# Decode block on one core: the last unit's first value piece ahead of the preceding unit's output mixing

## The chip, the cores and the metric

One core of a Trainium2 chip runs the kernel. The metric is device time in microseconds (us). A run's time is a little longer than the span of its profile, which begins with the first and ends with the last profiled instruction.

## The reference

Two batch rows of width 448 are normalised (`xn`). One branch is attention over the last 4096 positions of a key and value cache, with 16 query heads over 8 key heads of width 256. The other branch is a dense layer with the Mish activation. Both are added to the input:

```python
W = min(4096, max(256, Sk // 4))                 # 4096
q = (xn @ wq) -> (B, 16, 1, 256)
k, v = last W rows of the caches, each head used by 2 query heads
p = softmax(q k^T * 256 ** -0.5)
A = (p v) @ wo
h = xn @ w1 + b1
B = (h * tanh(softplus(h))) @ w2
out = x + A + B
```

Nearly all bytes are keys and values: 2 x 8 x 4096 x 256 bf16 numbers of each, 33.6 MB each. The page counts 77.78 MB moved in all.

## The kernel before, in words

The eight key heads are worked in U = 4 units of two heads, so that a unit holds four pairs of batch row and head. For unit u the keys come in two pieces of 4096 KB (`load_k`, tile `k`, two buffers). The values come in G = 4 pieces of 2048 KB (`load_v`, tile `v`, a ring of three buffers that the query weights and `w1` have used before). All of these large loads are issued by SyncE (SP), in the order of the program, on one queue. A load into a buffer waits on SP until the last reader of that buffer is done, and every load behind it waits too.

The parts of a unit:

- `turns(u, i)` (line 264): VectorE transposes a key piece into `kt`, in the four-byte form.
- `scores(u, i)` (line 329): TensorE (PE) multiplies query and keys, ScalarE (ACT) takes the exponent, and after the second half VectorE lays the weights `p` for the next product.
- `weigh(u)` (line 365): PE sums the weights with a matrix of ones into `dn`, VectorE makes the reciprocal `rec`.
- `values(u, g)` (line 382): 16 matmuls of `p` and value piece g into `pv`, each 32 weight columns by 512. Its last matmul frees the piece's buffer.
- `gather(u)` (line 401): ACT copies `pv` to `vs`, eight matmuls of 8 columns bring it to the transposed output `o`.
- `finish(u)` (line 434): VectorE scales by `rec` into `oT`.
- `relay(u)` (line 446): 16 small matmuls lay `oT` out afresh in `ox_ps`, ACT copies that to `ox`.
- `mix_early(u)` (line 468): eight matmuls of 448 columns with the output weights `wo` add the unit to the row accumulator `early`. Units 0 to 2 are added so.
- `carry()` (line 232): ACT copies `early` to `e_sb`, eight PE instructions put it in the final accumulator `acc`, four groups of 112 columns.

The last unit (u = 3) differs. Its first three value pieces go through `values`, and its fourth piece through `values_fixed` (line 420), which takes the values as the stationary operand and adds straight to `o`; this is 64 matmuls of 8 columns. `mix(3)` and `dense_out` then add to `acc` with 112-column matmuls (line 247). The second dense weight `w2` is loaded in four parts.

The loop body ends, for each unit u of the first three, with `scores(u + 1, 1)`, `weigh(u + 1)`, `relay(u)`, `mix_early(u)`. Below it stand SP's last loads and PE's last work:

```python
u = U - 1
load_v(u, 0)
load_v(u, 1)
load_wo(u)
load_v(u, 2)
load_v(u, 3, 0, 24)
load_v(u, 3, 24, T)
for part in range(len(w2_parts)):
    load_w2(part)
carry()
for g in range(G - 1):
    values(u, g)
```

With three buffers in the ring, value piece 3 of the last unit goes into the buffer that held piece 0 of the same unit. So `load_v(3, 3, 0, 24)` waits on SP for the last matmul of `values(3, 0)`; the second part of that piece and the four parts of `w2` are behind it in SP's program. The engines' programs run in the order written out here; nothing is reordered by a planner.

Of the kernel before, what the change touches and what calls it, by code (L numbers as in the profile page):

```python
# [17 lines left out]
def kernel(  # L18
# [29 lines left out]
    U = Hkv // KU  # L48
# [43 lines left out]
    def load_k(u, r):  # L92
        t = k_pool.tile([P, RK * KE], BF16, tag="k", name="k")
        src = kview[u][:, s0:, :].rearrange("j (c t) d -> c j (t d)", c=C)
        nc.sync.dma_start(out=t[:], in_=src[:, :, r * RK * KE : (r + 1) * RK * KE])  # L95
        k_t[u, r] = t

    def load_v(u, g, lo=0, hi=T):
        if lo == 0:
            v_t[u, g] = ring("v")  # L100
        t = v_t[u, g]
        src = vview[u][:, s0:, :].rearrange("j (g x t) d -> g x j (t d)", g=G, x=C)
        nc.sync.dma_start(  # L103
            out=t[:, lo * Dh : hi * Dh], in_=src[g, :, :, lo * Dh : hi * Dh]
        )

    def load_wo(u):
        w = wo_pool.tile([P, KU, rep, 2 * D], BF16, tag="wo", name="wo")
        if u < U - 1:
            nc.sync.dma_start(  # L110
                out=w[:].rearrange("p k h e -> p (k h e)"),
                in_=A_wo.rearrange("(k u y i) d -> u y k (i d)", k=KU, u=U, i=8)[u],
            )
        for k2 in range(KU if u == U - 1 else 0):
            r0 = (u + U * k2) * rep * Dh
            nc.sync.dma_start(
                out=w[:, k2, :, :],
                in_=A_wo[r0 : r0 + rep * Dh, :].rearrange("(h p c) d -> p h (c d)", h=rep, p=P),
            )
        wo_t[u] = w  # L120
# [111 lines left out]
    def carry():  # L232
        e_sb = small.tile([P, 2 * Dh], FP32, tag="vs", name="e_sb", bufs=1)[0:Bsz, 0:D]
        nc.scalar.copy(out=e_sb, in_=early[:])
        for g in range(G):
            nc.tensor.matmul(
                acc[32 * g : 32 * g + Bsz, :],
                lhsT=id2[:],
                rhs=e_sb[:, g * DG : (g + 1) * DG],
                start=True,  # L240
                stop=False,
                skip_group_check=True,
            )
# [20 lines left out]
    def turns(u, i):  # L264
        t = k_t.pop((u, i))
        for r in range(RK):
            nc.vector.transpose(  # L267
                out=kt[i][:, :, :, r, :],
                in_=t[:, r * KE : (r + 1) * KE].bitcast(FP32).rearrange(
                    "p (a c j) -> p a c j", c=P // (R * J), j=J  # L270
                ),
            )
# [56 lines left out]
    def scores(u, i):  # L329
        if i == 0:  # L330
            state["ex"] = small.tile([P, T, 2, NH, RK * J], BF16, tag="ex", name="ex", bufs=1)
        ex = state["ex"]
        sc = ps_sc.tile([P, T, 2, RK * J], FP32, tag="sc", name="sc")
        nc.tensor.matmul(  # L334
            sc[:].rearrange("p t c m -> p (t c m)"),
            lhsT=ident[:],
            rhs=mneg[:].rearrange("p a j -> p (a j)"),
            start=True,
            stop=False,
            skip_group_check=True,  # L340
        )
        for n in range(NB):
            for e in range(2):
                for w in range(4):
                    nc.tensor.matmul(  # L345
                        sc[32 * w : 32 * (w + 1)].rearrange("p t c m -> p t (c m)"),
                        lhsT=qd[:, u, 2 * n + e, :, :].rearrange("p g q -> p (g q)"),
                        rhs=ktm[i][:, n, e, :, 16 * w : 16 * (w + 1)],
                        start=False,
                        stop=(n == NB - 1 and e == 1),  # L350
                        skip_group_check=True,
                    )
        nc.scalar.activation(out=ex[:, :, :, i, :], in_=sc[:], func=ACT.Exp, scale=scale)  # L353
        if i == NH - 1:
            for h in range(NH):
                nc.vector.transpose(  # L356
                    out=p_t[h][:].rearrange("p g t q -> p t g q"),
                    in_=ex[:, h * TH : (h + 1) * TH].rearrange(
                        "p t c i m -> p t (c i m)"
                    ).rearrange("p t (g q) -> p t g q", g=G),  # L360
                )
# [20 lines left out]
    def values(u, g):  # L382
        if g == 0:
            state["v", u] = ps_v.tile([P, 2, Dh], FP32, tag="v", name="pv")
        pv = state["v", u]
        v = v_t.pop((u, g))
        for k in range(T // 2):
            a, b = k // 2, k % 2
            w = 2 * (a % 2) + b
            nc.tensor.matmul(  # L390
                pv[32 * w : 32 * (w + 1), :, :].rearrange("p x d -> p (x d)"),
                lhsT=p_t[a // 4][:, g, 4 * (a % 4) : 4 * (a % 4) + 4, :].rearrange(
                    "p t q -> p (t q)"
                ),
                rhs=v[:, 2 * k * Dh : (2 * k + 2) * Dh],
                start=(g == 0 and a < 2),
                stop=(g == G - 1 and a >= 6),
                skip_group_check=True,
            )

    def gather(u, last=True):
        pv = state.pop(("v", u))
        sb = small.tile([P, 2, Dh], FP32, tag="vs", name="vs", bufs=1)
        nc.scalar.copy(  # L404
            out=sb[:].rearrange("p x d -> p (x d)"), in_=pv[:].rearrange("p x d -> p (x d)")
        )
        po = ps_o.tile([P, 2, NQ], FP32, tag="o", name="o")
        for x in range(2):
            for c in range(2):
                nc.tensor.matmul(  # L410
                    po[:, c, :],
                    lhsT=sb[:, x, c::2],
                    rhs=sel[:, x, :],
                    start=(x == 0 and c == 0),
                    stop=(last and x == 1),
                    skip_group_check=True,
                )
        state["o", u] = po
# [27 lines left out]
    def relay(u):  # L446
        oT = state.pop(("oT", u))
        ox_ps = ps_m.tile([P, 4, 2, Bsz], FP32, tag="m", name="ox_ps")
        for h in range(rep):
            rows = slice(h * 64, (h + 1) * 64)  # L450
            for y in range(4):
                for k in range(KU):
                    nc.tensor.matmul(
                        ox_ps[rows, y, :, :],
                        lhsT=hot[:, k, y, :, :].rearrange("p q k -> p (q k)"),
                        rhs=oT[:, :, k * rep + h, :],
                        start=(y == 0 and k == 0),
                        stop=(y == 3 and k == KU - 1),
                        skip_group_check=True,
                    )  # L460
        ox = small.tile([P, 8, Bsz], BF16, tag="ox", name="ox")
        nc.scalar.copy(  # L462
            out=ox[:].rearrange("p i b -> p (i b)"),
            in_=ox_ps[:].rearrange("p y c b -> p (y c b)"),
        )
        state["ox", u] = ox

    def mix_early(u):
        ox = state.pop(("ox", u))
        w = wo_t.pop(u)[:].rearrange("p k h (c d) -> p (k h c) d", c=2)  # L470
        for i in range(8):
            nc.tensor.matmul(  # L472
                early[:],
                lhsT=ox[:, i, :],
                rhs=w[:, i, :],
                start=False,
                stop=(u == U - 2 and i == 7),
            )
# [87 lines left out]
    for u in range(U - 1):  # L566
        load_k(u + 1, 0)
        load_v(u, 0)
        load_v(u, 1)
        load_k(u + 1, 1)  # L570
        load_v(u, 2)
        load_v(u, 3)
        load_wo(u)
        turns(u + 1, 0)
        values(u, 0)
        values(u, 1)
        scores(u + 1, 0)
        turns(u + 1, 1)
        values(u, 2)
        values(u, 3)  # L580
        gather(u)
        finish(u)
        scores(u + 1, 1)
        weigh(u + 1)
        relay(u)
        mix_early(u)
    u = U - 1
    load_v(u, 0)
    load_v(u, 1)
# [3 lines left out]
    load_v(u, 3, 24, T)  # L593
    for part in range(len(w2_parts)):
        load_w2(part)
    carry()
    for g in range(G - 1):
        values(u, g)
    u = U - 1
    gather(u, last=False)  # L600
    values_fixed(u, G - 1, 0, 24)
# [45 lines left out]
```

The softmax here doesn't subtract the row's maximum and nothing guards it: scores larger than these inputs give would overflow.

## Time and profile before

| what | value |
|---|---|
| time, median of 3 runs | 194.07 us (193.81 to 194.4) |
| time of the profiled execution | 194.2 us |
| its span | 192.0 us |
| PE busy | 88.5 us (46%) |
| VectorE busy | 89.3 us (47%) |
| ACT busy | 12.3 us (6%) |
| HBM read | 77.67 MB, 405 GB/s over the span |
| SP's value loads, waiting for a DMA to land | 82.9 us in 12 waits |
| SP's value loads, waiting for PE | 33.2 us in 13 waits |
| last matmul of `values(3, 0)` ends | 175.86 us |
| `load_v(3, 3, 0, 24)` issued | 175.88 us |

How to read it: no compute engine is busy for half of the span, and the DMA engines are busy in nearly all of it. Busy time is a mean over the span; what a change is worth is read from the stretch in which it stands, here the last 25 us. In the view of stretches of time, each row gives a stretch, its length, each engine's busy time with the number of instructions, then the granted clock of PE, the busy share of the 16 DMA engines and what they moved. A DMA packet is counted there where it starts, so that a share can pass 1.

### The profile page before, as it was taken

The numbers are of one execution on the slowest core, as the hardware profiler recorded it, in microseconds if no ns is written. First come the engines' busy times: TensorE is split into PE (matmuls) and PEld (weight loads), VectorE is DVE, ScalarE is ACT, GpSimd is POOL, SyncE is SP. The second block draws the span as 40 slices with busy tenths as digits, with TensorE's granted clock in tenths as the row PEclk, the third lists the DMA queues.
The fourth block names the chain that finished last, engine by engine and source line by source line (L and its number), as shares of the span: only waits on it lengthen the run. The fifth ranks groups of instructions, "written<-read, shape, count | busy, mean of one in ns | idle before, by whom it ended". The sixth has DMA issues, their size and how long they took to land.

```text
span 192.0 us, 1986 instructions
## 1 busy us (share of the span) xinstructions
PE 88.5 (46%) x870; PEld 37.1 (19%) x873; DVE 89.3 (47%) x81; ACT 12.3 (6%) x23; POOL 4.0 (2%) x16
## 2 busy tenths in 40 slices
PE   0301554553238023866354034964380038788472
PEld 0100121520112001412111011511130014222261
DVE  5629544965960295029910691059700970130001
ACT  3000121001001000110001001010001001101101
POOL 8000000000000000000000000000000000000000
PEclk9999999558556755567558555585567555675855
DMA  6999998999999999999999999999999999997990
GB/s 219 437 386 434 492 437 360 452 420 420 423 440 437 427 425 417 443 434 423 447 440 396 413 424 480 423 393 430 478 430 393 416 432 435 401 415 294 311 412 15
DMA packets 5871, 77.78 MB, mean 405 GB/s; under 512 B 868, under 2 KB 1640, under 8 KB 2408
## 3 DMA queue, kind: packets, MB, share of 16 engines
q1 hardware_dynamic: 5588, 77.66, 96.0%
q8 instruction: 6, 0.10, 0.2%
q10 hardware_dynamic: 276, 0.01, 0.1%
q14 instruction: 1, 0.01, 0.0%
HBM read 77.67 MB, written 0.00 MB: 405 GB/s over the span
## 4 chain that ended last, share of the span: by engine, by line
DMA 79%; PE 11%; DVE 3%; issue 3%; SPq 2%; ACT 1%; DVEq 0%; ACTq 0%
DMA v<-in_A_v_cache_dram 58%; DMA k<-in_A_k_cache_dram 15%; DMA w<-in_B_w_dram 5%; PE pv L390 5%; DVE kt L267 2%; PE sc L345 2%; PE early L472 1%; PE o L410 1%; DVE p L356 1%; SPq L103 1%; SPq L544 1%; SPq L132 1%; SPq L95 1%; ACT ex L353 0%; ACT vs L404 0%
## 5 line engine op out<-in xcount | busy, mean ns | idle before, releaser
L267 DVE STREAM_TRANSPOSE kt<-k 128x4096 f32<-128x4096 f32 x16 | 70.1, 4420 | 40.7 <-DMA k<-in_A_k_cache_dram 40.6
L390 PE MATMUL pv<-v,p 128*32 128x512 bf16 x240 | 27.3, 608 | 56.7 <-DMA v<-in_A_v_cache_dram 56.7
L345 PE MATMUL sc<-kt,qd 128*32 128x512 bf16 x256 | 26.4, 582 | 4.6 <-DVE kt L267 2.3
L390 PEld LDWEIGHTS <-p 128*32 128x32 bf16 x240 | 8.7, 128 | 73.7 <-issue 66.0
L437 DVE TENSOR_TENSOR oT<-o,rec 128x16 bf16<-128x16 f32 x4 | 0.7, 176 | 31.4 <-PE o L410 16.6
L356 DVE STREAM_TRANSPOSE p<-ex 128x512 bf16<-128x512 bf16 x8 | 5.2, 690 | 15.9 <-ACT ex L353 15.9
L345 PEld LDWEIGHTS <-qd 128*32 128x32 bf16 x256 | 8.4, 131 | 19.2 <-issue 16.9
L353 ACT ACTIVATE ex<-sc 128x512 bf16<-128x512 f32 x8 | 4.8, 597 | 74.6 <-PE sc L345 74.6
L289 PE MATMUL q_ps<-wq,xs 128*32 128x512 bf16 x28 | 3.4, 624 | 11.9 <-DMA wq<-in_A_wq_dram 11.9
L472 PE MATMUL early<-wo,ox 128*2 128x448 bf16 x24 | 7.8, 491 | 0.8 <-ACT ox L462 0.8
L410 PE MATMUL o<-sel,vs 128*128 128x8 f32 x32 | 6.7, 339 | 2.8 <-ACT vs L404 2.8
L410 PEld LDWEIGHTS o<-sel,vs 128*128 128x128 f32 x32 | 6.4, 293 | 6.0 <-ACT vs L404 6.0
L368 PE MATMUL dn<-p,ones 128*128 128x512 bf16 x8 | 3.1, 381 | 6.6 <-DVE p L356 6.6
L404 ACT COPY vs<-pv 128x512 f32<-128x512 f32 x4 | 2.3, 586 | 51.8 <-PE pv L390 51.8
L502 PE MATMUL h_ps<-xs,w 128*128 128x4 bf16 x49 | 2.8, 193 | 4.6 <-DMA w<-in_B_w_dram 4.6
L210 PE MATMUL xr_ps<-ident,xrows 2*128 2x2 bf16 x7 | 1.0, 182 | 6.7 <-DVE xrows L209 6.7
L502 PEld LDWEIGHTS <-w 128*128 128x128 bf16 x49 | 2.7, 152 | 5.2 <-DMA w<-in_B_w_dram 5.2
L289 PEld LDWEIGHTS <-xs 128*32 128x32 bf16 x28 | 1.0, 125 | 13.9 <-issue 13.9
L376 DVE TENSOR_REDUCE rec<-dn 128x8 f32<-128x512 f32 x4 | 2.8, 692 | 1.9 <-PE dn L368 1.9
L425 PE MATMUL o<-p,v 128*128 128x8 bf16 x64 | 1.9, 168 | 2.5 <-DMA v<-in_A_v_cache_dram 2.5
L472 PEld LDWEIGHTS <-ox 128*2 128x2 bf16 x24 | 2.2, 102 | 4.1 <-issue 2.1
L334 PE MATMUL sc<-mneg,ident 128*128 128x512 bf16 x5 | 3.0, 591 | 0.0
(62 smaller groups left out, 36.3 us busy)
## 6 DMA issues: line engine op xcount, KB each, us to landing
k<-in_A_k_cache_dram SPq DMA_DIRECT2D x8, 4096.0 KB, 30.4
v<-in_A_v_cache_dram SPq DMA_DIRECT2D x15, 2048.0 KB, 27.3
wo<-in_A_wo_dram SPq DMA_DIRECT2D x3, 896.0 KB, 24.0
wq<-in_A_wq_dram SPq DMA_DIRECT2D x1, 2048.0 KB, 16.8
w<-in_B_w_dram SPq DMA_DIRECT2D x1, 1568.0 KB, 32.2
wq<-in_A_wq_dram SPq DMA_DIRECT2D x1, 1536.0 KB, 19.9
v<-in_A_v_cache_dram SPq DMA_DIRECT2D x1, 1536.0 KB, 7.1
wo<-in_A_wo_dram SPq DMA_DIRECT2D x2, 448.0 KB, 15.6
```

Of the source, the lines that this page charges most:

```text
L267: nc.vector.transpose(out=kt[i][:, :, :, r, :], in_=t[:, r * KE : (r + 1) * KE].bitcast(FP32).rearrange("p (a c j) -> p a c j", c=P // (R ...
L289: nc.tensor.matmul(q_ps[32 * u : 32 * (u + 1), :], lhsT=xs[:, s, :], rhs=wq_t[s][:, u * 512 : (u + 1) * 512], start=(s == 0), stop=(s == N ...
L334: nc.tensor.matmul(sc[:].rearrange("p t c m -> p (t c m)"), lhsT=ident[:], rhs=mneg[:].rearrange("p a j -> p (a j)"), start=True, stop=Fal ...
L345: nc.tensor.matmul(sc[32 * w : 32 * (w + 1)].rearrange("p t c m -> p t (c m)"), lhsT=qd[:, u, 2 * n + e, :, :].rearrange("p g q -> p (g q) ...
L353: nc.scalar.activation(out=ex[:, :, :, i, :], in_=sc[:], func=ACT.Exp, scale=scale)
L356: nc.vector.transpose(out=p_t[h][:].rearrange("p g t q -> p t g q"), in_=ex[:, h * TH : (h + 1) * TH].rearrange("p t c i m -> p t (c i m)" ...
L368: nc.tensor.matmul(dn[:].rearrange("p a q -> p (a q)"), lhsT=ones[:], rhs=p_t[i][:].rearrange("p g t q -> p (g t q)"), start=(i == 0), sto ...
L376: nc.vector.tensor_reduce(out=rec[:], in_=dn[:].rearrange("p a q -> p q a"), axis=AXIS.X, op=ALU.add)
L390: nc.tensor.matmul(pv[32 * w : 32 * (w + 1), :, :].rearrange("p x d -> p (x d)"), lhsT=p_t[a // 4][:, g, 4 * (a % 4) : 4 * (a % 4) + 4, :] ...
L410: nc.tensor.matmul(po[:, c, :], lhsT=sb[:, x, c::2], rhs=sel[:, x, :], start=(x == 0 and c == 0), stop=(last and x == 1), skip_group_check ...
L472: nc.tensor.matmul(early[:], lhsT=ox[:, i, :], rhs=w[:, i, :], start=False, stop=(u == U - 2 and i == 7),)
L502: nc.tensor.matmul(h_ps[:, i, :, :].rearrange("p k b -> p (k b)"), lhsT=w1_v[:, s, i, :], rhs=xs[:, s, 0 : 2 * Bsz], start=(s == 0), stop= ...
```

## The change

The last trip of the loop no longer issues `relay(2)` and `mix_early(2)`. Both are issued after `values(3, 0)`, and `carry()` with them, ahead of `values(3, 1)`:

```diff
@@ -582,8 +582,9 @@
         finish(u)
         scores(u + 1, 1)
         weigh(u + 1)
-        relay(u)
-        mix_early(u)
+        if u < U - 2:
+            relay(u)
+            mix_early(u)
     u = U - 1
     load_v(u, 0)
     load_v(u, 1)
@@ -593,9 +594,12 @@
     load_v(u, 3, 24, T)
     for part in range(len(w2_parts)):
         load_w2(part)
-    carry()
     for g in range(G - 1):
         values(u, g)
+        if g == 0:
+            relay(u - 1)
+            mix_early(u - 1)
+            carry()
     u = U - 1
     gather(u, last=False)
     values_fixed(u, G - 1, 0, 24)
```

On PE, 16 matmuls of `values(3, 0)` pass 16 of `relay(2)`, 8 of `mix_early(2)` and 8 of `carry`. The number of instructions on every engine stays the same. The orders of VectorE, ACT, GpSimd and SP stay as they were: the ACT copies `ox` and `e_sb` follow one another as before, and SP's loads have the same order and wait for the same things.

## The prediction

> **What bounds the kernel now.** I read three views: the chain that ended last, the waits of SP's queue, and half-microsecond stretches of the last 20 us. The chain, in order of time (start, length, what), from the place of the change on:
>
> ```profile
> 168.81 0.38 PE dn L368
> 169.19 0.51 PE ox_ps L453 x16
> 169.69 0.02 issue
> 169.72 0.18 ACT ox L462
> ...
> 169.94 2.86 PE early L472 x8
> ...
> 172.88 0.53 ACT e_sb L234
> ...
> 173.45 0.55 PE acc L236 x8
> 174.00 1.86 PE pv L390 x9
> 175.86 0.02 issue
> 175.88 0.54 SPq L103
> ...
> 178.26 10.52 DMA w<-in_B_w_dram
> ```
>
> The end hangs on the transfers of `w2`. They were issued behind a load (line 103) that SP could issue only when `values(3, 0)` had read its buffer. Those 16 matmuls stood behind 4.81 us (169.19 to 174.00) of relay, mix and carry. That SP waits for PE here, and PE for values, the waits say (total us, times, longest):
>
> ```profile
> SPq L103 <- PE pv L390: 33.2, 13, 10.4
> ```
>
> What the late issue costs the DMA engines (the last three columns: granted clock, DMA share, GB/s):
>
> ```profile
> 174.50:175.00 0.50, 0.50 (x12) 0.16 (x4) 0.00 (x0) 0.00 (x0) 0.00 (x0) 0.50 1.23 524
> 175.00:175.50 0.50, 0.50 (x8) 0.16 (x4) 0.00 (x0) 0.00 (x0) 0.00 (x0) 0.50 0.47 197
> 175.50:176.00 0.50, 0.50 (x8) 0.16 (x4) 0.00 (x0) 0.00 (x0) 0.00 (x0) 0.50 0.46 197
> 176.00:176.50 0.50, 0.50 (x12) 0.19 (x8) 0.00 (x0) 0.00 (x0) 0.00 (x0) 0.50 0.31 131
> 176.50:177.00 0.50, 0.50 (x12) 0.23 (x5) 0.00 (x0) 0.00 (x0) 0.00 (x0) 0.50 0.08 33
> 177.00:177.50 0.50, 0.39 (x8) 0.04 (x1) 0.00 (x0) 0.00 (x0) 0.00 (x0) 0.88 1.25 295
> ...
> 187.00:187.50 0.50, 0.24 (x16) 0.24 (x16) 0.00 (x0) 0.00 (x0) 0.00 (x0) 0.50 0.64 215
> 187.50:188.00 0.50, 0.30 (x16) 0.12 (x5) 0.00 (x0) 0.00 (x0) 0.00 (x0) 0.50 0.11 22
> 188.00:188.50 0.50, 0.00 (x0) 0.00 (x0) 0.00 (x0) 0.00 (x0) 0.00 (x0) 0.50 0.06 20
> ```
>
> The hole is not a clean one. More than half of the 16 engines stop near 175.4, the rest run out one after another until about 177.1: the transfer ahead, `v(3, 2)`, ends late on some engines. PE sees it only then:
>
> ```profile
> 177.60 1.05 PE L390 MATMUL pv<-v,p 128*32 128x512 bf16 x16 [0.21 <-DMA v<-in_A_v_cache_dram]
> ...
> 188.83 0.55 PE L247 MATMUL acc<-w,act_bf 128*2 128x112 bf16 x12 [1.03 <-DMA w<-in_B_w_dram]
> ```
>
> At the very end a share of 0.06 is one engine of 16: a single engine holds the last two parts of `w2`, and PE waits 1.03 us for it.
>
> **What the Trainium skill says.** "DMA: Bandwidth & Descriptors", section on queues, rings and completion order: one queue is a ring on each engine, consumed in ring order; so work queued early follows on each engine at once. The section on why a DMA increments its semaphore by 16 says that the engines finish independently and only the full count means landed. The trace agrees: `v(3, 2)` counts as landed at 177.6, though most engines stopped some 2 us before. "Runtime: NRT & Kernel Launch", section on instruction fetch mechanics: an engine's program is refilled in blocks of 16 KiB by a DMA queue of its own. The page lists 6 instruction packets on q8 with 0.10 MB, which is 16 KB each. I read the late engines, and the single one at the end, as those that had to fetch such a block; that is an inference, as the views name no engine.
>
> **The change part by part.** No instruction is added or removed.
>
> *The values piece.* `dn` ends at 169.19. `v(3, 0)` was issued at 140.77 and took 24.6 us to land, so it is there at 165.4. `pv` is free since ACT's copy at 160.87, and `p` since 168.77. So `values(3, 0)` runs from 169.19 for 1.86 us (its time here at half clock; 1.05 us at full clock, as at 177.60). It ends at 171.05 at the latest, 4.81 us earlier.
>
> *SP.* `load_v(3, 3, 0, 24)` goes out at 171.1 instead of 175.88. The second part and the four parts of `w2` follow, 3.3 us of issue in all (175.88 to 179.22 in before), so that all six are queued by 174.4. They also need semaphores that `v(3, 1)` and the first half of `wo(3)` last used. The latter is the later one: issued 155.97, 15.6 us to land, 171.6. It bars the last part alone, which comes up at 174. All bytes are then queued before the first engine runs dry near 175.4. The cover is some 4 us wide: the first load could go out as late as 174 or so.
>
> *Relay, mix and carry* move 1.86 us later and take the same 4.81 us: 171.05 to 175.86. `values(3, 1)` begins at 175.9 as before, and PE is ready for `values(3, 2)` at 177.4 as before, where it waits for `v(3, 2)` until 177.6. ACT's two copies have nothing behind them until `vs` at 178.75. The buffers of `wo(2)`, `ox` and `e_sb` come free later, but nobody waits for them. Cost: nothing, with 0.2 us of cover; beyond that, each us is lost to `gather`, which is not the bound.
>
> *What is late next.* `v(3, 2)` is not moved, so the engine that finishes it at 177.1 goes on there. Behind it are 2048 KB of `v(3, 3)` and 1568 KB of `w2`, in all 3.70 MB, or 231 KB for each engine. In before these took three steps:
> - first part of `v(3, 3)`, 1.57 MB: 177.0 to 182.0 at a mean of 315 GB/s (ten stretches, 98 to 393), 5.0 us;
> - the other 2.13 MB at 404 GB/s (182.0 to 187.0): 5.3 us;
> - 0.4 us to land, and the single late engine, to 178.7 + 10.3 = 189.0 for the last part (the longest time to landing against its issue), some 1.25 us behind the others' 177.1 + 5.0 + 5.3 + 0.4 = 187.8.
>
> In after, the single late engine need not count. If its fetch falls on an engine that is not late with `v(3, 2)`, that engine has up to 1.7 us in hand (175.4 against 177.1), and the 1.25 us vanish.
>
> The slow first part is the unknown. If the stop and common restart make it slow, it takes 1.57 MB / 420 GB/s = 3.75 us, the rate of the stretches before the hole. If its 12-KB rows do, it stays at 5.0 us. I take 4.4: with engines out of step, the late ones have part of it to themselves. Then the last `w2` lands at 177.1 + 4.4 + 5.3 + 0.4 = 187.2, against 189.0: 1.8 us gained. The bounds are 186.55 (2.5 gained) and 187.8 (1.2 gained).
>
> *PE as the bound.* With `v(3, 3)` landing near 181.9, PE does 1.87 (line 425), 0.26 (VectorE and hand-over), 0.92 (`mix`), then 0.82, 0.54 and 0.55 for `dense_out`: 4.96 us, to 186.9, even with no pause. That is before 187.2 + 0.35, so DMA stays the bound, narrowly. `gather` at half clock would end by 182.1 (1.9, 0.6 and 1.9 from 177.6) and set 187.05.
>
> **Sum.** 1.8 us of the profiled execution's own 194.2 us: 192.4. Its span goes from 192.0 to 190.2. The profiled execution lies 0.13 us above the median of 194.07, within its runs' spread, so I leave the number as it is, rounded down to 192.3.
>
> **Rivals.**
> - *A, the forecast:* late engines carry on at once, fetch hidden; 191.7 to 193.0. Chance 0.64.
> - *B, the fetch hits a late engine:* then the 1.25 us stay. With the first part at 4.4 us the gain is 0.55; over its bounds, 0 to 1.25. Time 192.9 to 194.2, mean 193.6. For it: several engines are late, and one more fetch will come. Against: `v(3, 2)` ends on the late engines step by step, as if each had lost one fetch and none two. Chance 0.18, about half of it over 0.3% faster.
> - *C, the late engines don't matter:* if all ran level, 175.4 + 3.75 + 5.3 + 0.4 = 184.85, and PE's 186.5 to 187.0 would be the end; 191.5. Against: `v(3, 2)` itself is not issued earlier. Chance 0.06.
> - *D, slower:* the low rate of 177 to 182 is that of engines out of step, and as nothing brings them into step any more, it holds to the end. Place: DMA from 177.1. It decides below 3.70 MB / (189.0 - 0.4 - 177.1 us) = 322 GB/s; at 300 GB/s the last part lands at 189.8, 0.8 later: 195.0. For it: 315 GB/s was measured in this very stretch. Against: before the hole, with engines out of step too, it was over 400. Chance 0.07.
> - *E, it does not do what it says:* SP is held by something else, for example the landing of `v(3, 0)`, and issues as late as before: 194.2. Chance 0.05.
>
> **How the numbers follow.** 0.3% of 194 us, 0.58 us, is about what can be told from no change here. Faster: 0.64 + 0.06 + 0.12 of B (its larger part, as a fetch that is partly hidden falls there too) = 0.82. Within: the rest of B and E, 0.11. Slower: D, 0.07. The range reaches from C's 191.5 to B's upper part, 193.9; outside lie D, E and the last of B, some 0.16.
>
> **What would show it.** In the profile of the changed kernel: line 390 right after `dn` near 169.2; SP's load at 170.4 to 171.1, all six issues done by 174.5; no stretch between 175 and 177.5 with a DMA share under 0.8; `v(3, 2)` landing at 177.6 still; the 64 matmuls of line 425 starting near 181.3 to 182.2 in place of 183.02; no wait of a full microsecond for `w` ahead of the last matmuls. I'd be wrong if `v(3, 2)` landed later than 178 because the earlier engines' new traffic slows the late ones; if the stretch from 177 to 182 still moved some 315 GB/s and the last `w2` still landed on one engine alone; or if PE, and not `w2`, were what ends last.

## The result and the profile after

| | before | changed |
|---|---|---|
| median, us | 194.24 (4 runs) | 191.85 (4 runs, 191.77 to 191.99) |
| ratio to before | 1 | 0.987 (95% interval 0.9829 to 0.9911) |
| profiled execution, us | 194.2 | 191.77 |
| its span, us | 192.0 | 189.5 |
| load of the fourth value piece issued at | 175.88 | 171.21 |
| last part of `w2` landed at (its issue and its time to landing) | 189.0 | 186.3 |

The changed kernel is faster by 1.3%. A second set of six runs, shown with the experiments, gave 191.86 us and a ratio of 0.9879 (0.985 to 0.9908). The kernel before has two groups of runs, 53 of its 84 in all sets between 192.59 and 194.66 us and 31 between 194.82 and 195.8, so its median moves with their mix, while the ten runs of the changed kernel lie within 191.72 to 191.99.

The chain that ended last, of the changed kernel (start, length, what), beginning where `dn` ends:

```profile
168.16 1.17 PE dn L368 x2
169.34 1.86 PE pv L390 x16
171.20 0.02 issue
171.21 0.54 SPq L103
...
172.49 0.54 SPq L544
173.04 0.05 issue
173.09 12.37 DMA w<-in_B_w_dram
185.45 0.04 issue
185.49 0.54 PE acc L247 x11
```

Relay, mix and carry have left the chain: `pv` follows `dn` at once, and SP issues 4.67 us earlier. A part of `w2` now stands in the chain for 12.37 us (the second part), where one stood for 10.52 in before (the third). That is no loss: it is queued earlier and waits behind other bytes.

What PE waited for on the way, in the changed kernel:

```profile
177.55 1.05 PE L390 MATMUL pv<-v,p 128*32 128x512 bf16 x16 [0.21 <-DMA v<-in_A_v_cache_dram]
181.26 1.86 PE L425 MATMUL o<-p,v 128*128 128x8 bf16 x64 [0.81 <-DMA v<-in_A_v_cache_dram]
```

Half-microsecond stretches of the changed kernel (the last three columns: granted clock, DMA share, GB/s), at the place of the hole and at the end:

```profile
175.00:175.50 0.50, 0.33 (x1) 0.00 (x0) 0.00 (x0) 0.08 (x1) 0.00 (x0) 0.80 0.99 418
175.50:176.00 0.50, 0.01 (x1) 0.01 (x2) 0.00 (x0) 0.44 (x1) 0.00 (x0) 1.00 1.04 442
176.00:176.50 0.50, 0.50 (x12) 0.21 (x16) 0.00 (x0) 0.00 (x0) 0.00 (x0) 1.00 1.14 483
176.50:177.00 0.50, 0.50 (x16) 0.26 (x9) 0.00 (x0) 0.00 (x0) 0.00 (x0) 1.00 0.70 295
177.00:177.50 0.50, 0.34 (x8) 0.05 (x1) 0.00 (x0) 0.00 (x0) 0.00 (x0) 1.00 1.11 467
...
184.00:184.50 0.50, 0.39 (x24) 0.21 (x16) 0.00 (x0) 0.00 (x0) 0.00 (x0) 0.50 0.73 264
184.50:185.00 0.50, 0.50 (x28) 0.50 (x26) 0.00 (x0) 0.00 (x0) 0.00 (x0) 0.50 0.36 143
185.00:185.50 0.50, 0.25 (x15) 0.06 (x3) 0.00 (x0) 0.00 (x0) 0.00 (x0) 0.50 0.35 131
185.50:186.00 0.50, 0.50 (x16) 0.35 (x16) 0.00 (x0) 0.00 (x0) 0.00 (x0) 0.50 0.22 74
```

The hole is gone: the five stretches from 175 have a mean share of 1.0 (a packet counts where it starts, so 0.70 and 1.11 belong together). The end has a new look. From 184.5 on, about six of the 16 engines (0.36 of them) still work, for some 1.5 us, while the others have finished. Just as many worked on alone in the hole of before (a share of 0.46 and then 0.31, up to 176.5), so I take them for the engines that were late with `v(3, 2)`; the views name no engine. In before, the stop let the others wait for them.

The rate behind `v(3, 2)`, as one stretch of 5 us of each kernel, before first, then changed:

```profile
177.00:182.00 5.00, 2.55 (x32) 1.42 (x24) 0.00 (x0) 0.59 (x1) 0.00 (x0) 0.84 0.97 315
```

```profile
176.00:181.00 5.00, 3.50 (x48) 1.90 (x48) 0.00 (x0) 0.59 (x1) 0.00 (x0) 1.00 0.98 408
```

In both the engines were busy (0.97 and 0.98), but they moved 315 GB/s in one and 408 in the other. The packets of the trace say it row by row: the 128 rows of 12 KB took 0.61 us each in before, on the mean, and 0.465 in the changed kernel; for an engine's eight rows that is some 1.1 us. So a slow period followed the hole.

### The profile page after: what moved, and what is told of

Same layout as the page of the kernel before. It is cut to its first block, busy times and chain, and to the rows that moved or that the text cites. A ratio compares the mean times of both kernels' runs of the same rounds, so it can differ in the third digit from the quotient of the medians.

```text
span 189.5 us, 1989 instructions
## 1 busy us (share of the span) xinstructions
PE 93.9 (50%) x873; PEld 38.0 (20%) x873; DVE 89.2 (47%) x81; ACT 12.3 (7%) x23; POOL 4.0 (2%) x16
## 4 chain that ended last, share of the span: by engine, by line
DMA 81%; PE 9%; DVE 3%; issue 3%; SPq 2%; ACT 1%; DVEq 0%
DMA v<-in_A_v_cache_dram 59%; DMA k<-in_A_k_cache_dram 15%; DMA w<-in_B_w_dram 7%; PE pv L390 5%; DVE kt L267 2%; PE sc L345 2%; PE o L410 1%; PE acc L247 1%; PE dn L368 1%; SPq L103 1%; SPq L132 1%; SPq L95 1%; DVE p L356 0%; ACT ex L353 0%; ACT vs L404 0%
## 5 line engine op out<-in xcount | busy, mean ns | idle before, releaser
L390 PE MATMUL pv<-v,p 128*32 128x512 bf16 x240 | 26.2, 583 | 53.7 <-DMA v<-in_A_v_cache_dram 53.7
L345 PE MATMUL sc<-kt,qd 128*32 128x512 bf16 x256 | 28.2, 614 | 3.2 <-DVE kt L267 1.8
L472 PE MATMUL early<-wo,ox 128*2 128x448 bf16 x24 | 9.4, 570 | 0.8 <-ACT ox L462 0.8
L368 PE MATMUL dn<-p,ones 128*128 128x512 bf16 x8 | 4.3, 540 | 6.0 <-DVE p L356 6.0
L334 PE MATMUL sc<-mneg,ident 128*128 128x512 bf16 x8 | 4.8, 595 | 0.0
L453 PEld LDWEIGHTS <-hot 128*64 128x64 bf16 x48 | 2.0, 142 | 2.6 <-issue 2.6
```

The lines of the kernel that those rows point to most:

```text
L334: nc.tensor.matmul(sc[:].rearrange("p t c m -> p (t c m)"), lhsT=ident[:], rhs=mneg[:].rearrange("p a j -> p (a j)"), start=True, stop=Fal ...
L345: nc.tensor.matmul(sc[32 * w : 32 * (w + 1)].rearrange("p t c m -> p t (c m)"), lhsT=qd[:, u, 2 * n + e, :, :].rearrange("p g q -> p (g q) ...
L368: nc.tensor.matmul(dn[:].rearrange("p a q -> p (a q)"), lhsT=ones[:], rhs=p_t[i][:].rearrange("p g t q -> p (g t q)"), start=(i == 0), sto ...
L390: nc.tensor.matmul(pv[32 * w : 32 * (w + 1), :, :].rearrange("p x d -> p (x d)"), lhsT=p_t[a // 4][:, g, 4 * (a % 4) : 4 * (a % 4) + 4, :] ...
L472: nc.tensor.matmul(early[:], lhsT=ox[:, i, :], rhs=w[:, i, :], start=False, stop=(u == U - 2 and i == 7),)
```

## Experiments

The theory under test, "stop and restart": the time hangs on whether the last loads are queued before the DMA engines run dry, and on nothing else that the change does. Rivals: the order or the clock of PE; the amount of the delay, microsecond for microsecond; the shape of the transfer that follows.

### The wait taken away in the old order, and in the new

```diff
-            v_t[u, g] = ring("v")
+            if (u, g) == (U - 1, G - 1):
+                v_t[u, g] = k_pool.tile([P, RK * KE], BF16, tag="k", name="v")
+            else:
+                v_t[u, g] = ring("v")
```

The fourth piece lies in a key buffer; `values_fixed` reads the first KE columns of it. On the kernel before:

> The kernel before in its own order of work, but the fourth value piece of the last unit lies in a key buffer that is free by 158 us, so that SP's load waits for no value piece and goes out near 161. Theory 'stop and restart': the hole at 175 to 177 is gone and the time is that of the changed kernel, 191.5 to 192.1. Rival 'PE' (the order on PE or its clock brings the gain): 194.2, or the hole is gone and the end is not earlier by over 0.5 us.

On the changed kernel:

> The changed kernel with that same key buffer for the fourth value piece. If freeing the buffer earlier is all that the change does, it has nothing left to bring: the time is that of the kernel with the own buffer in the old order, 191.5 to 192.1, within 0.3 us. If the order on PE is worth something by itself, this one is faster than the other by over 0.5 us.

Measured: 191.71 us, ratio 0.9899 (0.986 to 0.9937), and 191.84 us, ratio 0.9904 (0.9871 to 0.9937). SP's issues in the first of them (start, length):

```profile
160.94 1.25 SPq L106 DMA_DIRECT2D v<-in_A_v_cache_dram  x2
162.29 9.69 SPq L547 DMA_DIRECT2D w<-in_B_w_dram  x4
```

Issued 15 us earlier, in the old order of PE, the kernel takes what the changed one takes, and the new order adds nothing to it. The order on PE is worth something only through the buffer that it frees. The rival "PE" falls.

### How early is early enough

Three kernels put the load at other times. The changed kernel with relay alone back ahead of `values(3, 0)`:

```diff
+        relay(u)
         if u < U - 2:
-            relay(u)
             mix_early(u)
...
         if g == 0:
-            relay(u - 1)
             mix_early(u - 1)
             carry()
```

> The changed kernel, but relay(2) goes back ahead of values(3, 0), with its copy on ScalarE; mix and carry stay behind. SP's load goes out some 0.6 us later than in the changed kernel, near 171.8. Theory 'stop and restart': still 3 us before the engines run dry, so the time is that of the changed kernel, 191.8 within 0.3. Rival 'amount of delay' with no free cover: 0.5 us slower, 192.4.

The kernel before with relay and five matmuls of mix ahead, and three of mix and carry behind (`mix_early` takes bounds for this):

```diff
         relay(u)
-        mix_early(u)
+        mix_early(u, 0, 8 if u < U - 2 else 5)
...
-    carry()
     for g in range(G - 1):
         values(u, g)
+        if g == 0:
+            mix_early(u - 1, 5, 8)
+            carry()
```

> The changed kernel, but relay(2) and five of the eight matmuls of mix_early(2) stay ahead of values(3, 0); three of mix_early and carry stay behind. SP's load goes out near 173.9, 2.7 us later than in the changed kernel and about 1.1 earlier than with carry alone moved, which cost 1.7 us. Theory 'stop and restart': it is still in time, or just so, for first bytes at 175.2, and costs nothing or little: 191.7 to 192.3. Rival 'amount of delay': 1 us or more is lost, 192.8 to 193.2.

The kernel before with only carry behind:

```diff
-    carry()
     for g in range(G - 1):
         values(u, g)
+        if g == 0:
+            carry()
```

> The kernel before, with only carry moved behind values(3, 0); relay and mix stay ahead of it. SP's load should go out near 174.7 us, 1.2 earlier than in before and 3.5 later than in the changed kernel. Theory 'stop and restart' (the gain is that bytes are queued before the DMA engines run dry, and that no common restart follows): the first engines run dry near 175.4 and the new bytes start near 176.0, so about ten engines pause for 0.6 us and the late ones not at all; the stretch from 176 to 181 should move 380 GB/s or more, and the time be 191.9 to 192.8. Rival 'amount of delay' (each us of earlier issue is a us of time, until 2.4 are gained): 1.2 us gained, 193.0. Rival 'PE' (the gain is PE's order or clock at the end): as before, 194.2.

| load issued at (profiled execution) | kernel | median, us | ratio to before (95%) |
|---|---|---|---|
| 160.94 | old order, own buffer | 191.71 | 0.9899 (0.986 to 0.9937) |
| 171.21 | changed | 191.85 | 0.987 (0.9829 to 0.9911) |
| 172.06 | mix and carry behind | 191.82 | 0.9881 (0.9833 to 0.9928) |
| 173.09 | three of mix and carry behind | 192.28 | 0.9898 (0.9855 to 0.994) |
| 175.04 | carry behind | 193.54 | 0.9955 (0.9919 to 0.999) |
| 175.88 | before | 194.24 | 1 |

It is a step with a slope, not a line: 11 us of further delay from the first row to the third cost nothing, the next 1 us costs 0.3 to 0.5, and between 173.09 and 175.88 the rest of the gain is lost. The rival "amount of delay" falls for early issues and is not far off for late ones, with 2 us lost over the last 2.8 us of delay. How the loss divides over the last rows is not settled, since the issue time in the row of carry belongs to an execution of 194.57 us, 1 us above the median, and its twelve runs reach down to 191.59, where the changed kernel is. My own expectation for carry alone was 191.9 to 192.8, as the late engines have no pause in it; that was too good by 0.4 us (by its ratio, 193.2) to 0.7 us (by its median). The missing part is in the rate, and the kernel with five matmuls ahead shows it (columns as above):

```profile
175.00:176.00 1.00, 0.61 (x12) 0.20 (x5) 0.00 (x0) 0.00 (x0) 0.00 (x0) 1.00 1.04 401
176.00:177.00 1.00, 0.00 (x0) 0.00 (x0) 0.00 (x0) 0.00 (x0) 0.00 (x0) 1.00 0.93 389
177.00:178.00 1.00, 0.42 (x8) 0.23 (x11) 0.00 (x0) 0.00 (x0) 0.00 (x0) 1.00 1.05 406
178.00:179.00 1.00, 0.63 (x12) 0.12 (x4) 0.00 (x0) 0.27 (x1) 0.00 (x0) 1.00 1.00 332
179.00:180.00 1.00, 0.63 (x4) 0.64 (x4) 0.00 (x0) 0.31 (x1) 0.00 (x0) 0.75 0.84 279
```

There is no hole here: the share stays near 1 from 175 to 179. Yet from 178 on the rate falls to 332 and then 279 GB/s. A load that comes just in time still costs something, so a full stop of all engines is not what makes the slow period.

### Is it the shape of what follows?

The old order with the fourth piece in one DMA, so in 16-KB rows:

```diff
-    load_v(u, 3, 0, 24)
-    load_v(u, 3, 24, T)
+    load_v(u, 3)
```

> The kernel before, but the fourth value piece of the last unit is loaded by one DMA (16-KB rows) in place of two (12-KB and 4-KB rows); the stop at 175 to 177 stays. It asks why the first 1.57 MB after the stop moved at 315 GB/s. Theory 'common restart' (whatever follows a stop is slow for some 5 us): the stretch from 177 to 182 moves 300 to 340 GB/s again, and the time is 194 to 195. Rival '12-KB rows in step' (only this shape is slow, when all engines begin it together): the stretch moves 400 or more, w2 lands 1.3 us earlier, and the time is 192.7 to 193.3, though values_fixed begins later, as it waits for the whole piece.

Measured: 193.1 us, ratio 0.9927 (0.9892 to 0.9963); from 177 to 182 the engines moved 390 GB/s. That is the rival's time, and nearly its rate. But in this run `values(3, 0)` was at full clock, and the load went out at 174.56, 1.3 us earlier than in before, so the earlier issue could have done it. The two kernels without `mix(3)`, shown below, settle that: they load the piece in 12-KB and 4-KB rows, their loads went out at 174.94 and 174.74, and they are as slow as before. The same stretch with 16-KB rows, then in those two:

```profile
177.00:182.00 5.00, 2.92 (x24) 2.14 (x23) 0.00 (x0) 0.59 (x1) 0.00 (x0) 0.71 0.97 390
177.00:182.00 5.00, 2.71 (x24) 1.92 (x23) 0.00 (x0) 0.58 (x1) 0.00 (x0) 0.78 0.98 327
177.00:182.00 5.00, 2.90 (x24) 2.11 (x23) 0.00 (x0) 0.58 (x1) 0.00 (x0) 0.74 0.95 310
```

So 16-KB rows suffer less than 12-KB rows do.

The old order with `w2` first, in the buffer that `values(3, 0)` frees, and the fourth piece behind it in the key buffer:

```diff
-            state["w2"] = k_pool.tile([P, RK * KE], BF16, tag="k", name="w2")
+            state["w2"] = ring("w2")
...
+    for part in range(len(w2_parts)):
+        load_w2(part)
     load_v(u, 3, 0, 24)
     load_v(u, 3, 24, T)
-    for part in range(len(w2_parts)):
-        load_w2(part)
```

> The kernel before, in its order of work, with two buffers exchanged and SP's last loads turned round: the four parts of w2 go into the ring buffer that values(3, 0) frees, and follow it, and the fourth value piece goes into the free key buffer behind them. The stop near 175 to 177 stays, but what follows it is w2, rows that lie end to end in memory. It asks whether the slow stretch belongs to the stop or to the value piece. Theory 'common restart': w2 is slow too, the 3 us after the restart move 300 to 340 GB/s. Rival 'the value piece's rows': w2 moves at 390 or more, and the value piece, if anything, is slow behind it. The time says little, as the 64 matmuls of values_fixed and mix now come after the last byte: 194.5 to 196.5 is expected either way.

Measured: 196.64 us, ratio 1.0118 (1.0079 to 1.0156), just above what was expected; the load of `w2` went out at 174.92. The rate after the restart, with `w2` first:

```profile
176.00:177.00 1.00, 0.00 (x0) 0.00 (x0) 0.00 (x0) 0.00 (x0) 0.00 (x0) 1.00 0.59 182
177.00:178.00 1.00, 0.40 (x8) 0.23 (x11) 0.00 (x0) 0.00 (x0) 0.00 (x0) 1.00 0.88 351
178.00:179.00 1.00, 0.64 (x12) 0.12 (x4) 0.00 (x0) 0.25 (x1) 0.00 (x0) 1.00 1.04 368
179.00:180.00 1.00, 0.61 (x5) 0.62 (x5) 0.00 (x0) 0.33 (x1) 0.00 (x0) 0.92 0.88 331
```

The mean from 177 to 180 is 350 GB/s, between what the two theories gave, and in each full stretch under the 390 of the rival. Put together: every transfer that followed a late issue was slower than the 408 GB/s of the changed kernel, by some 4% (16-KB rows), 14% (`w2`, where a share of 0.93 is a part of it) and 20 to 24% (12-KB rows). The same 12-KB rows ran at 408 when they had been queued in time. So the shape sets how much. What sets whether is less sharp than the name "late issue" says: in the kernel with `w2` first, the fourth piece went out at 177.26 and its first rows began 3 us later, at 180.3, and still the engines, at a share of 0.98, moved only 370 GB/s from 181 to 185. These are single traces. What inside the DMA system makes the rows slow was not found, and stays open.

### The single late engine at the end

In before, one engine landed the last two parts of `w2` a good microsecond behind the others, and I took it for the one that fetched PE's last program block. The kernel before without `mix(3)`, which leaves out the last unit's product with `wo`:

```diff
     finish(u)
-    mix(u)
```

> The kernel before without mix(3): the last unit's product with the output weights is left out, 32 matmuls on PE (with their weight loads 64 instructions) that lie beside DMA in before. Theory 'instruction fetch' (the single engine that lands the last two parts of w2 some 1.25 us late is the one that fetched PE's last program block): with 64 instructions fewer behind it the fetch starts later, when w2 has landed or nearly, so the last part lands at 187.8 and the time is near 193.0; the instruction packet then lies after 187.5. If the fetch still starts before 187, no change is expected from either side. Rival 'slow engine or small last parts': the last part lands at 189.0 as before and the time is 194.0.

And with idle matmuls ahead of the first `weigh`, which restore the length of the program:

```diff
+        for i in range(32 if u == 0 else 0):
+            nc.tensor.matmul(
+                dn[:, 0, :], lhsT=ones[:], rhs=p_t[0][:, 0, 0, :], start=True, stop=True
+            )
```

> The same without mix(3), and with 32 short matmuls of no use (64 instructions) ahead of the first weigh, where PE has time, so that the program is as long again as that of before and its last block begins at the old distance from the end. Theory 'instruction fetch': the packet is back at 184 to 187 and one engine lands late, 1.2 us behind the others; the time is near 194.2, slower by about 1 us than without the padding. Rival: the two differ by less than 0.3 us.

Measured: 194.12 us, ratio 0.9992 (0.9968 to 1.0017) without the padding, and 193.58 us, ratio 0.9952 (0.993 to 0.9974) with it. The direction was the opposite of what I expected, as the instruction packet didn't go where I had put it. Without `mix(3)` it lies between 185 and 187, as in before, so that this kernel could not decide. With the padding there are two, one between 174 and 176, inside the hole, and one after 188, when all has landed. PE's last lines, without padding and with it:

```profile
186.79 0.54 PE L247 MATMUL acc<-w,act_bf 128*2 128x112 bf16 x16 [0.25 <-DMA w<-in_B_w_dram]
188.09 0.51 PE L247 MATMUL acc<-w,act_bf 128*2 128x112 bf16 x12 [0.77 <-DMA w<-in_B_w_dram]
```

```profile
187.49 1.09 PE L247 MATMUL acc<-w,act_bf 128*2 128x112 bf16 x28 [0.27 <-DMA w<-in_B_w_dram]
```

With the padding PE no longer waits ahead of the last parts. But that is no proof that they came earlier: PE was 0.7 us later here (187.49 against 186.79), and it began the last 12 matmuls at 188.03, against 188.09 without the padding. Nor does the time decide. The difference of 0.5 us between the medians comes mostly from 8 of the 20 unpadded runs, at 194.99 us and more, while no padded run is above 194.25; the other twelve have a median of 193.69 us, and the two profiled executions, 193.43 and 193.36 us, are alike. What speaks for the fetch is in the packets. In before the instruction packet runs from 186.44 to 187.33, and from 187.3 to 188.1 four rows of 1792 bytes, each begun where the last ended and so on one engine, take 0.19 to 0.20 us each, where such rows take 0.074 elsewhere; that engine then works on alone to the end. Without `mix(3)` it is the same (packet from 186.04 to 187.0, and two such rows of 0.20 from 187.0 on), and with the padding, where no packet falls on the tail, no row is slow. So the fetch as the cause of the lone engine is supported by the packets, while its worth in time is not shown.

### The same padding on the changed kernel

> The changed kernel with the 32 short matmuls of no use (64 instructions) ahead of the first weigh, as in the padded one before, so that PE's program blocks are fetched at other times. Theory 'stop and restart': a fetch that delays one engine by about 1.2 us is hidden, since late engines 1.5 us behind decide the end: 191.8 within 0.3. Rival 'every fetch near the end counts': the time moves by 0.5 us or more, either way.

Measured: 191.37 us, ratio 0.9843 (0.9802 to 0.9885). That is outside what my theory gave (191.5 to 192.1), by little. As the changed kernel had been measured in another set, both were run again side by side:

> The changed kernel itself, as the neighbour of the padded one on the same chip: 191.6 to 192.1.

> The changed kernel with the 32 short matmuls of no use, a second time, beside the changed kernel itself. In the trace of the changed kernel PE does one matmul of the last two parts of w2 at 186.07 and the next at 186.48, with no wait that the profile shows; in the padded one they run on. Theory 'program block' (the edge of a program block falls there, and the padding moves it): 0.3 to 0.5 us faster than its neighbour, 191.3 to 191.5. Rival 'chip or day': no difference over 0.2 us.

Measured: 191.86 us, ratio 0.9879 (0.985 to 0.9908), and padded 191.41 us, ratio 0.9855 (0.9823 to 0.9888); the runs are 191.72 to 191.92 and 191.16 to 191.59, with no overlap. PE's last two groups in the timeline, without padding and with it:

```profile
185.59 0.83 PE L247 MATMUL acc<-w,act_bf 128*2 128x112 bf16 x17 [0.24 <-DMA w<-in_B_w_dram]
186.60 0.45 PE L247 MATMUL acc<-w,act_bf 128*2 128x112 bf16 x11 [0.18 <-issue]
```

```profile
185.51 1.11 PE L247 MATMUL acc<-w,act_bf 128*2 128x112 bf16 x28 [0.25 <-DMA w<-in_B_w_dram]
```

Without the padding PE pauses before 186.60 with no wait that the profile shows; with it the 28 matmuls run through and end near 186.62, against 187.05. This 0.4 us is the difference, 0.08 of it an earlier start. It is a pause in PE's own program, not in a transfer; that it is the edge of a program block is inferred from what moves it. It lies behind the same matmul in six other traces of unpadded kernels, those of the two with an own buffer and of all with the load at other times among them. It is missing in the padded ones, but also in before and in the kernel with one DMA for the piece, so the place in the program alone does not make it. The padded version is the fastest of the study, though by an accident of length that any later edit can undo.

## Why the prediction was right

The forecast was 192.3 us, and 191.85 was measured. By its steps:

- *The values piece and SP's issue.* `values(3, 0)` ran from 169.27 and ended at 171.20; the load went out at 171.21 and all six were issued by 174.45. Forecast: 171.05 at the latest, 171.1 and 174.4. Right but for 0.15 us, as `dn` ran at half clock here and ended at 169.34.
- *Relay, mix and carry at no cost.* PE waited for `v(3, 2)` until 177.55 as before, and relay, mix and carry lay ahead of it. Right. The cover was given as some 4 us and as reaching to an issue at 174, which do not agree, for 174 is only 2.9 us behind 171.1. It is 1 to 2 us: 172.06 is free, 173.09 costs 0.3 to 0.5.
- *No stretch under a share of 0.8.* By the letter this sign failed, with 0.70 at 176.5; together with the 1.11 behind it there is no hole.
- *The late engines decide.* `v(3, 2)` was seen by PE at 177.55 against 177.60, so it didn't move, and about six engines worked on alone at the end. Right; rival C, that they don't matter, needed the last landing at 184.85, and it was at 186.3. That late engines are those that had to fetch a block stayed an inference, but it fits in number: in before, six instruction packets (five of q8, one of q14) lie between the start of the span and the hole.
- *The first part's rate.* I took 4.4 us, between 3.75 and 5.0. This is the term that was mis-sized: at 408 GB/s its 1.57 MB take 3.85 us. The 64 matmuls of line 425 began at 181.26, at the early edge of the stretch named. The reason for 4.4, that engines out of step keep part of the slowness, was wrong; transfers queued in time had none of it.
- *The fetch.* One instruction packet falls between 184 and 185 in the changed kernel, too. The last `w2` landed at 186.3 on several engines together, with no lone one behind; the 1.25 us vanished, as said, and rival B did not come. The landing was forecast for 187.2, with 186.55 as the fast bound; it was earlier than that bound by 0.25 us.
- *PE close behind.* 186.9 was worked out for an uninterrupted PE with the fourth piece landing near 181.9. The piece came 0.7 us earlier, and PE's last matmul still ended at 186.93, by a pause of 0.4 us that I hadn't seen coming. So the sign "if PE, and not `w2`, were what ends last" came true for that last bit; without the pause the gain would have been 2.8 us.
- *Rival D*, that engines out of step stay slow, is refuted: they moved 408 GB/s out of step. *E* is refuted by the issue at 171.21.

The sum then reads: 1.25 us from the lone engine, 1.15 us from the rate of the first part (5.0 to 3.85), and some 0.3 us that no term accounts for, which makes 2.7 us at the last landing (189.0 to 186.3); PE's pause took some of it back, and 2.5 us of span are left. The mechanism was right. That the total fell on the fast bound of 2.5 us is in part luck, since the early landing and the pause, neither of them forecast, nearly cancel.

## What to carry to other kernels

Where the DMA queue is the bound, look for stretches in which the engines run out, and follow SP back to the instruction that frees the buffer; moving that one reader ahead of work that nobody waits for gained some 2 us here. By the sum above the idle time itself was not the gain, since ten engines now only finish earlier and the six late ones set the end; the gain was what followed the hole, the slow rows and the lone engine. Queue the next loads a few microseconds before the last ones end, as a load that is just in time already costs: here an issue at 172.06, 3.3 us before the first engines ran dry in before (175.4), was free, and one at 173.09, 2.3 us before, was not. And read the last microseconds by number of engines: a share of 0.06 is one late engine, and 0.36 is six.

## What the runs showed that I had not expected

- After a late issue the DMA engines are busy but slow: 315 GB/s at a share of 0.97 for 5 us, against 408 at 0.98. It happens with the share never under 0.8 too (332 and 279 GB/s in the kernel with five matmuls ahead). Only the transfer that comes first was slow in before: of the rows behind its 12-KB ones, those of 4 KB took 0.159 us in before and 0.161 in the changed kernel.
- 32 matmuls of no use, at 8 columns each, make the changed kernel 0.45 us faster, with a pause in PE's program gone from the path.
- The time at which the buffer comes free depends on PE's clock. In before the load went out at 175.88, with `values(3, 0)` at half clock (1.86 us). In the kernel without `mix(3)`, the same up to there, it was 174.94, with the clock at 1.0 from 173. Once the load is early, this no longer reaches the end: four runs of the changed kernel lie within 191.77 to 191.99 at mean clocks from 0.656 to 0.757.
